# Cross-attention with state tokens and a SiLU feed-forward on one core: the instruction order of batch 0 rearranged

## The chip, the cores and the metric

The kernel runs on one core of a Trainium2 chip. Its engines are TensorE (PE: matmuls and transposes through an identity), VectorE (DVE), ScalarE (ACT: SiLU, exponentials, copies), GpSimd (POOL) and SyncE (SP, which issues transfers here). The metric is the device time of one execution in microseconds (us), lower being better. Nine runs of the kernel before gave a median of 216.46 us, from 216.35 to 216.77.

## The reference, cut to what matters

```python
# B, H, S, Ns, D = 8, 8, 512, 32, 64;  w_in 512 x 2048, w_out 2048 x 512, all float32
scores = (x @ state.T) / 8                    # per batch and head
xread  = softmax(scores) @ state              # 512 rows a batch
sread  = softmax((state @ x.T) / 8) @ x       # 32 rows a batch
y = concat([xread, sread], axis=2)            # 544 rows a batch, heads side by side: 512 wide
h = y @ w_in
out = (h * sigmoid(h)) @ w_out                # 4352 rows of 512
```

## The kernel before, in words

**Two products are folded.** For the 512 xread rows of a batch the kernel never forms xread. It multiplies the state into `w_in` once a batch (`W1`, `w1_mms`, line 449: 32-row pieces of four heads packed into the 128 rows of an output, for two groups of heads), and then h = W1 x softmax. `W1[b]` has two groups (`hg`) of 128 x 2048 bf16. A `w1_mms` for 512 columns is eight small matmuls into two PSUM banks; `w1_out` (471) copies the two banks to SBUF, by the two engines given (`both` is DVE for group 0, ACT for group 1).

**Tiles.** `d_ff` has 16 blocks of 128, called steps `ft`. G1 of step ft (`emit_G1`, 523; step number k = 16 b + ft; `g1_first`, 489, for the very first) is two 512-wide matmuls of W1 and the transposed softmax `aT`, into one of two PSUM banks of the pool `psH`, and one SiLU on ACT that writes `g`. G2 (548) adds `g` of a step times `w_out` into the output of one of four token tiles `tt`, 16 steps each. Each output has a PSUM bank: tiles 0 and 1 of batch 0 have `o0` and `o1`, tiles 2 and 3 have `a0` and `a1`. `store` (564) copies a finished output to SBUF and sends it off. G1 of step 1 alone borrows `a1` (line 512). `bank()` (74) hands out the tags in the list `banks` in turn; for W1 pieces in batch 0 these are `a2` and `a3`. A buffer that is asked for again makes PE wait until its reader is done.

**Order.** Nothing is scheduled by a planner: each engine runs its instructions in the order in which the program emits them. `upto(k)` (592) emits G1 up to step k. In batch 0, loop at 643, `LEAD0` says how far G1 runs ahead of G2, and `W0` gives the steps at which W1 of batch 0 gets its next 512 columns; `ready` limits G1 to columns that exist. Steps 5 and 9 make columns 0 to 511 and 512 to 1023 of batch 1's W1 (652); step 4 places batch 1's state (650). G2 of tile 3 runs with the others for steps 0 to 2, then stops; three of its steps are issued at step 12 and the rest from 685 on, as PE's work while batch 1's softmax is made. That softmax: `cast_x` (127) makes x bf16 in `x_rows`, `pe_transpose_x` (243) transposes it on PE, `scores` (297), `exps` (312, ACT), `norm` (369: sum and reciprocal on DVE, product on POOL for group 0 and on DVE for group 1), `pe_transpose_a` (393). After it come the last two W1 pieces of batch 1 and its G1.

**The start.** x of batch 0 comes in two loads on SP. Its second half (heads 4 to 7) is cast by ACT (row groups c 2, 3) and POOL (c 0, 1) at 268 and 269. `keep_busy` (161) emits idle matmuls. ACT must load a table of functions before the first EXP and before the first SiLU; the instruction on `warm` before a section brings the load forward.

**Loads.** Weights, states and x of batches 1 to 3 are issued by POOL, in program order with POOL's own work.

From line 700 on, batches 1 to 7 follow in a loop, and then the 256 sread rows.

Of the kernel before, what the change touches and what calls it, by code (L numbers as in the profile page):

```python
# [9 lines left out]
BF16 = mybir.dt.bfloat16  # L10
# [15 lines left out]
NFT = DF // 128  # L26
# [15 lines left out]
def kernel(  # L42
# [8 lines left out]
    nc = tc.nc  # L51
# [75 lines left out]
    def cast_x(b, eng, c0=0, nc_=4, h0=0, nh=H):  # L127
        if b < 2:
            x_nat[b] = padded(b)
        elif b not in x_nat:  # L130
            x_nat[b] = xpool.tile([128, 4, 4, 128], BF16, tag="x_nat", name=f"x_nat{b}")
        copy(
            eng,
            x_nat[b][:, ds(c0, nc_), ds(h0 // 2, nh // 2), :].rearrange(
                "p c k (u d) -> p c k u d", u=2
            ),
            x_f[b % 2][:, ds(h0, nh), ds(c0, nc_), :].rearrange("p (k u) c d -> p c k u d", u=2),
        )
# [12 lines left out]
    def load_w_out(g0, n):  # L151
        nc.gpsimd.dma_start(w_out_sb[:, ds(g0, n), :], wout_re[:, ds(g0, n), :])

    def copy(eng, dst, src):
        if eng is nc.scalar:
            nc.scalar.activation(dst, src, func=COPY, bias=0.0)  # L156
        else:
            eng.tensor_copy(dst, src)  # L158


    def keep_busy(n, pool, tag):
        ps = pool.tile([128, 512], FP32, tag=tag, name="ps_busy")
        for _ in range(n):
            nc.tensor.matmul(  # L164
                ps[:], busy[:, 0:128], busy[:], start=True, stop=True, skip_group_check=True
            )
# [36 lines left out]
    def transpose_one_state(st):  # L203
        ps = bank([128, 2, 2, 2, 16], BF16, "ps_st1")
        nc.tensor.transpose(
            ps.rearrange("p g k u m -> p (g k u m)"), st.rearrange("p v d -> p (v d)"), ident[:]
        )
        return ps
# [8 lines left out]
    def place_one_state(b, ps, eng):  # L217
        for u in range(2):
            by_n = slots_of(b)[u].rearrange("p g (k m v) -> p g k m v", m=16, v=2)
            for v in range(2):  # L220
                copy(eng, by_n[:, :, 0:3:2, :, v], ps[ds(64 * v, 64), :, :, u, :])
# [21 lines left out]
    def pe_transpose_x(b, hg, nb=2, new=bank, engs=(nc.vector, nc.scalar), only=None):  # L243
        if b not in xT:
            xT[b] = xtpool.tile([128, 4, 4, 128], BF16, tag="xT", name=f"xT{b}")
        m = 4 // nb
        for u in range(nb) if only is None else only:
            ps = new([128, m, 2, 128], BF16, "ps_xt")
            for i in range(m):
                for j in range(2):  # L250
                    nc.tensor.transpose(  # L251
                        ps[:, i, j, :],
                        x_nat[b][:, m * u + i, 2 * hg + j, :],
                        ident[:],
                    )
            copy(engs[u], xT[b][:, ds(m * u, m), ds(2 * hg, 2), :], ps[:])
# [9 lines left out]
    o_tags = ["o0", "o1"]  # L266
    new_o = lambda sh, dt, nm: psO.tile(sh, dt, tag=o_tags.pop(), name=nm)
    cast_x(0, nc.scalar, 2, 2, 4, 4)
    cast_x(0, nc.gpsimd, 0, 2, 4, 4)
    pe_transpose_x(0, 0, 2, new_o, (nc.vector, nc.vector))  # L270

    st_x = pers.tile([128, 8, B, 4, 2, 2], BF16)

# [116 lines left out]
            aT[b][:, hg, :, :], an[b, hg][:].rearrange("p c s n -> p (c s n)")  # L390
        )

    def pe_transpose_a(b, hg, eng, new=bank, c0=0, n=4):
        ps = new([128, n, 128], BF16, "ps_at")
        for c in range(n):
            nc.tensor.transpose(ps[:, c, :], an[b, hg][:, c0 + c, :, :], ident[:])
        copy(eng, aT[b][:, hg, ds(c0, n), :], ps[:])


    xm_ps = {}  # L400
# [48 lines left out]
    def w1_mms(b, cols, new=bank):  # L449
        pss = {}  # L450
        if b not in W1:
            W1[b] = wpool.tile([128, 2, DF], BF16, tag="W1", name="W1")
        for f, n in cols:
            for hg in range(2):
                pss[f, hg] = new([128, 512], FP32, "ps_w1")
            for s in range(4):
                for hg in range(2):
                    h = HEAD_OF_SLOT[hg][s]
                    r = 64 * (h % 2)
                    nc.tensor.matmul(  # L460
                        pss[f, hg][ds(32 * s, 32), 0:n],
                        stT[ds(r, 64), b, h // 2, s % 2, :],
                        w_in_sb[ds(r, 64), h // 2, ds(f, n)],
                        start=True,
                        stop=True,
                        tile_position=(r, 32 * s),
                        skip_group_check=True,
                    )
        return pss

    def w1_out(b, cols, engs, pss, at=0):
        for f, n in cols:
            for hg in range(2):
                copy(engs[hg], W1[b][:, hg, ds(f + at, n)], pss[f, hg][:, ds(at, n)])

    def w1_cols(b, cols, engs, new=bank):
        w1_out(b, cols, engs, w1_mms(b, cols, new))
# [114 lines left out]
    def upto(k):  # L592
        while done[0] < min(k, (B + 1) * NFT):
            emit_G1(done[0])
            done[0] += 1

    new_h = lambda sh, dt, nm: psH.tile(sh, dt, tag="h1", name=nm)
    keep_busy(1, psH, "h1")
    scores(0, 0)
    exps(0, 0)  # L600
    keep_busy(1, psH, "h1")
    pe_transpose_x(0, 1, 2, new_h, (nc.vector, nc.scalar))
    norm(0, 0)
    scores(0, 1, 2)
    exps(0, 1)
    norm(0, 1, ((nc.vector, 0, 4),), 2)
    pss0 = w1_mms(0, [(0, 128)])
    nc.scalar.activation(warm[:], busy[:, 0:1], func=SILU, bias=0.0)
    w1_out(0, [(0, 128)], (nc.scalar, nc.scalar), pss0)
    load_w_in(1024)  # L610
    load_w_out(8, 4)
    load_w_in(1536)
    for hg in range(2):
        load_x(1, 4 * hg, 4)
    load_w_out(12, 4)
    load_states()
    load_x(2)
    for i in range(3):
        ones_beside_x(i, nc.gpsimd)
    keep_busy(3, psH, "h1")  # L620
    pss0 = w1_mms(0, [(128, 384)])
    keep_busy(2, psH, "h1")
    new_o = lambda sh, dt, nm: psO.tile(sh, dt, tag=o_tags.pop(), name=nm)
    o_tags[:] = ["o0", "o1"]
    for c in (0, 2):
        pe_transpose_a(0, 0, nc.scalar, new_o, c, 2)
    for c in (0, 2):
        pe_transpose_a(0, 1, nc.vector, bank, c, 2)
    upto(1)
    w1_out(0, [(128, 128)], (nc.vector, nc.vector), pss0)  # L630
    w1_out(0, [(128, 256)], (nc.vector, nc.vector), pss0, 128)
    upto(2)

    banks[:] = ["a2", "a3"]
    turn[0] = 0
    W0 = {2: (512, 512), 6: (1024, 512), 10: (1536, 512)}
    LEAD0 = [2, 2, 2, 2, 2, 3, 2, 3, 3, 2, 2, 4, 4]  # L640
    F3 = 3
    ready = 4
    for ft in range(NFT - 2):
        upto(min(ft + LEAD0[min(ft, 12)], ready))
        if ft in W0:
            w1_cols(0, [W0[ft]], both)
            ready = sum(W0[ft]) // 128
        if ft == 4:
            place_one_state(1, transpose_one_state(st1_n), nc.vector)
        if ft in (5, 9):  # L650
            w1_chunks(1, ({5: 0, 9: 1}[ft],), both)
        if ft == 11:
            for hg in range(2):
                cast_x(1, nc.vector, 0, 4, 4 * hg, 4)
            load_x(3)
        if ft == 12:
            nc.scalar.activation(warm[:], busy[:, 0:1], func=EXP, bias=0.0)
            for i in range(F3, F3 + 3):
                G2(0, 3, i)
            pe_transpose_x(1, 0, 1, engs=(nc.vector,))  # L660
            pe_transpose_x(1, 1, 1, engs=(nc.vector,))
        for tt in range(4 if ft < F3 else 3):
            G2(0, tt, ft)
    F3 += 3
    banks[:] = ["a2", "a3", "a0", "a1"]
    turn[0] = 0
    scores(1, 0, new=new_h)
    scores(1, 1, new=new_h)
    exps(1, 0)
    exps(1, 1)  # L670
    for tt in (0, 2, 1):
        G2(0, tt, 14)
        G2(0, tt, 15)
        if tt != 1:
            store(0, tt, nc.scalar)
    nc.scalar.activation(warm[:], busy[:, 0:1], func=SILU, bias=0.0)
    norm(1, 0)
    norm(1, 1, ((nc.vector, 0, 4),))
    tail_tags = ["a2", "a3", "a0", "o0"]

    def tail_bank(shape, dtype, name):
        tag = tail_tags.pop(0)
        return (psO if tag == "o0" else psA).tile(shape, dtype, tag=tag, name=name)

    for ft in range(F3, NFT):
        if ft == 12:
            pe_transpose_a(1, 0, nc.vector, new_h)
        if ft == 14:
            pe_transpose_a(1, 1, nc.vector, new_h)
            store(0, 1, nc.vector)  # L690
            cols = [(1024, 512), (1536, 512)]
            pss1 = w1_mms(1, cols, tail_bank)
            w1_out(1, cols, (nc.vector, nc.vector), pss1)
            for i in (2, 3):
                for c in range(4):
                    cast_x(i, nc.gpsimd, c, 1)
            transpose_states()
            transpose_x(2)
            upto(NFT + 2)
        G2(0, 3, ft)  # L700
    upto(NFT + 3)
    store(0, 3, nc.vector)

# [100 lines left out]
```

The softmax here doesn't subtract the row's maximum and nothing guards it: scores larger than these inputs give would overflow.

## Time and profile before

| what | value |
|---|---|
| median of nine runs | 216.46 us |
| the profiled execution | 216.41 us |
| its span, first to last instruction | 214.6 us |
| granted TensorE clock, mean | 1.000 |
| PE busy | 205.5 us (96%), 1549 instructions |
| ACT busy | 139.6 us (65%), 244 instructions |
| DVE busy | 76.5 us (36%), 170 instructions |
| POOL busy | 39.6 us (18%), 61 instructions |
| G2 outside of `o_a`, 128x512 | 483 records, mean 379 ns |
| G1 of batches 0 to 7, 128x512 | 242 records, mean 379 ns |
| SiLU and its forms | 143 records, mean 573 ns |
| table loads on ACT | 1283 ns each |

The profile is of one execution. Matmuls are pipelined, so that the 379 ns of one are not the time from one to the next; a few per cent of the matmul records are missing. "Slices" are the span cut into 40 equal parts, each digit the busy share in tenths. The "chain" goes back from the last instruction to what released it, and so on. A "hole" in this text is time on PE in which no matmul started that could have.

### The profile page before, as it was taken

The numbers are of one execution on the slowest core, as the hardware profiler recorded it, in microseconds if no ns is written. First come the engines' busy times: TensorE is split into PE (matmuls) and PEld (weight loads), VectorE is DVE, ScalarE is ACT, GpSimd is POOL, SyncE is SP. The second block draws the span as 40 slices with busy tenths as digits, with TensorE's granted clock in tenths as the row PEclk, the third lists the DMA queues.
The fourth block names the chain that finished last, engine by engine and source line by source line (L and its number), as shares of the span: only waits on it lengthen the run. The fifth ranks groups of instructions, "written<-read, shape, count | busy, mean of one in ns | idle before, by whom it ended". The sixth has DMA issues, their size and how long they took to land.

```text
span 214.6 us, 3867 instructions
## 1 busy us (share of the span) xinstructions
PE 205.5 (96%) x1549; PEld 96.8 (45%) x1575; DVE 76.5 (36%) x170; ACT 139.6 (65%) x244; POOL 39.6 (18%) x61
## 2 busy tenths in 40 slices
PE   7899999999899999999999999999999999999993
PEld 2443344445344444444444444444444444466653
DVE  3734247855951156106610551135312415200011
ACT  3866578699657976699459956786675366634410
POOL 8683013702420122004110402000200000000000
PEclk9999999999999999999999999999999999999999
DMA  5999999696649567374657295114310211011112
GB/s 187 206 202 206 293 273 340 172 234 214 89 99 264 157 107 195 88 208 105 167 80 240 76 156 127 49 52 104 94 53 16 91 49 53 0 49 49 52 49 98
DMA packets 42914, 28.66 MB, mean 134 GB/s; under 512 B 28048, under 2 KB 37776, under 8 KB 42896
## 3 DMA queue, kind: packets, MB, share of 16 engines
q1 hardware_dynamic: 36720, 20.65, 37.3%
q0 software_dynamic: 5888, 7.64, 17.1%
q8 instruction: 12, 0.20, 0.4%
q10 hardware_dynamic: 288, 0.13, 0.2%
q14 instruction: 6, 0.05, 0.1%
HBM read 17.43 MB, written 8.91 MB: 123 GB/s over the span
## 4 chain that ended last, share of the span: by engine, by line
PE 86%; DVE 5%; ACT 3%; DMA 2%; issue 1%; POOL 0%; POOLq 0%
PE o L555 47%; PE h L514 25%; PE ps_w L460 4%; PE h L535 3%; PE o_a L555 2%; DMA x_f<-in_x_dram 2%; PE o_part L577 2%; DVE W L158 2%; ACT exp_nat L317 1%; DVE rs L376 1%; PE ps_xt L251 1%; PE ps_sr L412 1%; DVE rc L428 1%; PE ps_scT L329 1%; ACT L317 1%
## 5 line engine op out<-in xcount | busy, mean ns | idle before, releaser
L555 PE MATMUL o<-w_out_sb,g 128*128 128x512 bf16 x483 | 129.3, 379 | 1.8 <-issue 1.1
L546 ACT ACTIVATE g<-h 128x512 bf16<-128x512 f32 (+1 forms) x143 | 81.4, 573 | 37.0 <-PE h L514 23.0
L555 PEld LDWEIGHTS <-g 128*128 128x128 bf16 x528 | 50.0, 98 | 57.6 <-issue 3.2
L514 PE MATMUL h<-aT,W 128*128 128x512 bf16 x242 | 72.2, 379 | 0.5 <-ACT g L546 0.3
L158 DVE COPY o_sb<-o 128x512 f32<-128x512 f32 x15 | 10.4, 691 | 89.2 <-PE o L555 85.1
L514 PEld LDWEIGHTS <-W 128*128 128x128 bf16 x254 | 24.5, 98 | 31.8 <-issue 2.0
L158 DVE CAST W<-ps_w 128x512 bf16<-128x512 f32 (+2 forms) x37 | 23.0, 648 | 25.3 <-PE ps_w L460 25.3
L156 ACT ACTIVATE W<-ps_w 128x512 bf16<-128x512 f32 (+1 forms) x31 | 16.4, 570 | 12.6 <-PE ps_w L460 12.6
L158 POOL CAST x_nat<-x_f 128x512 bf16<-128x512 f32 x24 | 14.6, 650 | 33.6 <-issue 22.7
L156 ACT ACTIVATE o_sb<-o 128x512 f32<-128x512 f32 x16 | 9.6, 597 | 12.1 <-PE o L555 8.9
L359 POOL TENSOR_TENSOR an<-e,rcn 128x512 bf16<-128x512 bf16 x5 | 7.6, 1519 | 49.1 <-DVE rcn L357 49.1
L460 PE MATMUL ps_w<-w_in_sb,stT 64*32 64x512 bf16 (+2 forms) x264 | 11.1, 375 | 0.7 <-DVE W L158 0.7
L555 PE MATMUL o_a<-w_out_sb,g 128*128 128x512 bf16 x32 | 10.2, 379 | 0.1
L535 PE MATMUL h<-xmT,w_in_sb 128*128 128x256 bf16 x64 | 9.6, 273 | 0.0
L535 PEld LDWEIGHTS <-w_in_sb 128*128 128x128 bf16 x64 | 6.3, 98 | 3.9
L164 PE MATMUL ps_busy<-busy 128*128 128x512 bf16 x15 | 5.7, 487 | 1.2 <-DVE warm L171 1.2
L460 PEld LDWEIGHTS <-stT 64*32 64x32 bf16 x264 | 3.4, 89 | 7.3 <-issue 4.9
L748 ACT ACT_TABLE_LOAD x5 | 6.4, 1283 | 0.1
L343 ACT ACTIVATE eT<-ps_scT 128x512 bf16<-128x512 f32 x10 | 5.4, 595 | 1.6 <-PE ps_scT L329 1.6
L379 POOL TENSOR_TENSOR an<-exp_nat,rc 128x512 bf16<-128x512 bf16 x3 | 3.1, 1050 | 17.6 <-ACT eT L343 10.7
L356 DVE TENSOR_REDUCE rs<-e 128x32 f32<-128x1024 bf16 x5 | 6.1, 1211 | 0.2 <-DMA e<-eT 0.2
L108 POOL DMA_DIRECT2D x_f<-in_x_dram x4 | 3.3, 841 | 12.5 <-DVE x_rows L158 10.3
(76 smaller groups left out, 104.0 us busy)
## 6 DMA issues: line engine op xcount, KB each, us to landing
out_dram<-o_sb SPq DMA_DIRECT2D x33, 256.0 KB, 2.4
x_f<-in_x_dram SPq DMA_DIRECT2D x4, 1024.0 KB, 6.3
x_f<-in_x_dram POOLq DMA_DIRECT2D x2, 1024.0 KB, 13.5
w_in_sb<-in_moe_w_in_dram POOLq DMA_DIRECT2D x3, 512.0 KB, 10.5
w_out_sb<-in_moe_w_out_dram POOLq DMA_DIRECT2D x3, 512.0 KB, 12.3
x_f<-in_x_dram SPq DMA_DIRECT2D x2, 512.0 KB, 4.9
x_f<-in_x_dram POOLq DMA_DIRECT2D x2, 512.0 KB, 15.2
w_out_sb<-in_moe_w_out_dram POOLq DMA_DIRECT2D x2, 256.0 KB, 7.8
```

The costliest lines, as they stand in the source:

```text
L156: nc.scalar.activation(dst, src, func=COPY, bias=0.0)
L158: eng.tensor_copy(dst, src)
L164: nc.tensor.matmul(ps[:], busy[:, 0:128], busy[:], start=True, stop=True, skip_group_check=True)
L343: nc.scalar.activation(t[:, hg], scT_ps[hg][:], func=EXP, bias=0.0, scale=SCALE)
L356: nc.vector.tensor_reduce(rs[:], e2[b][:], axis=AX, op=ADD)
L359: eng.tensor_tensor(a[:, hg], e2[b][:, hg], rc[:, hg].to_broadcast([128, 4, 4, NS]), op=MULT)
L460: nc.tensor.matmul(pss[f, hg][ds(32 * s, 32), 0:n], stT[ds(r, 64), b, h // 2, s % 2, :], w_in_sb[ds(r, 64), h // 2, ds(f, n)], start=True, ...
L514: nc.tensor.matmul(h_ps[k][:], W1[b][:, hg, ds(128 * ft, 128)], aT[b][:, hg, :, :], start=(hg == 0), stop=(hg == 1), skip_group_check=True,)
L535: nc.tensor.matmul(ps[:, 0:256], w_in_sb[:, kt, ds(128 * ft, 128)], xmT[:, :, kt].rearrange("p t n b -> p t (n b)"), start=(kt == 0), stop ...
L546: nc.scalar.activation(g[:, 0:n], ps[:, 0:n], func=SILU, bias=0.0)
L555: nc.tensor.matmul(outs[tt][:], gt[b * NFT + ft][:, ds(128 * tt, 128)], w_out_sb[:, ft, :], start=(ft == 0), stop=(ft == NFT - 1), skip_gr ...
L748: nc.scalar.activation(warm[:], busy[:, 0:1], func=SILU, bias=0.0)
```

## The change

The order and the buffers of batch 0, and of the passage to batch 1, are rewritten:

- POOL casts row group 0 of the second half of x, DVE row group 1 (in its queue between the first two and the third copy to `xT`), ACT groups 2 and 3 as before.
- ACT copies the first 128 columns of W1 ahead of its load of the SiLU table. The next pieces use banks `a2` and `a3`; the transposed softmax of batch 0 uses `o1`, `a0`, `a1`, `o0`, and its copies, and those of W1 columns 128 to 255, are shared by DVE and ACT.
- The last load of `w_out` is issued as two.
- Batch 1's state is placed at step 1. W1 of batch 1 gets columns 0 to 511 at step 4, and 512 to 1023 at step 6, directly behind batch 0's piece; the latter goes into the two `psH` banks.
- G2 of tile 3 starts at the end of step 1 and keeps up to step 6; steps 7 to 11 stand between the transposes and scores of batch 1, 12 and 13 between the transposes of its softmax, 14 and 15 behind its first two G1.
- The last piece of batch 0's W1 is at step 10. At step 11 come G1 12 and 13, the casts and first transposes of x of batch 1, G1 14 and 15, and the EXP table. Tiles 0 to 2 do steps 12 to 15 behind the scores, in twos, tile by tile.

From the sums over batch 1 on, the program is the same. The diff, cut to its core:

```diff
     cast_x(0, nc.scalar, 2, 2, 4, 4)
-    cast_x(0, nc.gpsimd, 0, 2, 4, 4)
+    cast_x(0, nc.gpsimd, 0, 1, 4, 4)
     pe_transpose_x(0, 0, 2, new_o, (nc.vector, nc.vector))
+    cast_x(0, nc.vector, 1, 1, 4, 4)
...
-    pss0 = w1_mms(0, [(0, 128)])
+    w1_cols(0, [(0, 128)], (nc.scalar, nc.scalar))
     nc.scalar.activation(warm[:], busy[:, 0:1], func=SILU, bias=0.0)
-    w1_out(0, [(0, 128)], (nc.scalar, nc.scalar), pss0)
...
-    load_w_out(12, 4)
+    load_w_out(12, 2)
+    load_w_out(14, 2)
...
     keep_busy(3, psH, "h1")
+    banks[:] = ["a2", "a3"]
+    turn[0] = 0
     pss0 = w1_mms(0, [(128, 384)])
     keep_busy(2, psH, "h1")
...
     for c in (0, 2):
-        pe_transpose_a(0, 0, nc.scalar, new_o, c, 2)
+        ps_a = (psO, psA)[c // 2].tile(
+            [128, 2, 128], BF16, tag=("o1", "a0")[c // 2], name="ps_at"
+        )
+        at_mms(ps_a, 0, 0, c, 2)
+        copy(both[c // 2], aT[0][:, 0, ds(c, 2), :], ps_a[:])
     for c in (0, 2):
-        pe_transpose_a(0, 1, nc.vector, bank, c, 2)
+        ps_a = (psO, psA)[c == 0].tile(
+            [128, 2, 128], BF16, tag=("o0", "a1")[c == 0], name="ps_at"
+        )
+        at_mms(ps_a, 0, 1, c, 2)
+        copy(nc.vector, aT[0][:, 1, ds(c, 2), :], ps_a[:])
+    w1_out(0, [(128, 128)], both, pss0)
     upto(1)
-    w1_out(0, [(128, 128)], (nc.vector, nc.vector), pss0)
...
-    LEAD0 = [2, 2, 2, 2, 2, 3, 2, 3, 3, 2, 2, 4, 4]
-    F3 = 3
+    W1_AT = {4: 0, 6: 512}
+    LEAD0 = [2, 2, 2, 2, 2, 3, 2, 1, 3, 3, 2, 3]
+    T3 = {1: (0, 1), 2: (2,), 3: (3,), 4: (4,), 5: (5,), 6: (6,)}
...
-    for ft in range(NFT - 2):
-        upto(min(ft + LEAD0[min(ft, 12)], ready))
+    for ft in range(12):
+        upto(min(ft + LEAD0[ft], ready))
+        if ft == 1:
+            place_one_state(1, transpose_one_state(st1_n), nc.vector)
         if ft in W0:
-            w1_cols(0, [W0[ft]], both)
+            pss = w1_mms(0, [W0[ft]])
+            if ft in W1_AT:
+                pss1 = w1_mms(1, [(W1_AT[ft], 512)], new_h)
+            w1_out(0, [W0[ft]], both, pss)
+            if ft in W1_AT:
+                w1_out(1, [(W1_AT[ft], 512)], both, pss1)
             ready = sum(W0[ft]) // 128
-        if ft == 4:
-            place_one_state(1, transpose_one_state(st1_n), nc.vector)
-        if ft in (5, 9):
-            w1_chunks(1, ({5: 0, 9: 1}[ft],), both)
+        elif ft in W1_AT:
+            w1_cols(1, [(W1_AT[ft], 512)], both)
         if ft == 11:
             for hg in range(2):
                 cast_x(1, nc.vector, 0, 4, 4 * hg, 4)
             load_x(3)
-        if ft == 12:
+            pe_transpose_x(1, 0, 1, engs=(nc.vector,))
+            upto(16)
             nc.scalar.activation(warm[:], busy[:, 0:1], func=EXP, bias=0.0)
-            for i in range(F3, F3 + 3):
-                G2(0, 3, i)
-            pe_transpose_x(1, 0, 1, engs=(nc.vector,))
-            pe_transpose_x(1, 1, 1, engs=(nc.vector,))
-        for tt in range(4 if ft < F3 else 3):
+        for tt in range(3):
             G2(0, tt, ft)
...
+            if ft == 7 and tt == 0:
+                upto(9)
+        for i in T3.get(ft, ()):
+            G2(0, 3, i)
+    pe_transpose_x(1, 1, 1, engs=(nc.vector,))
+    G2(0, 3, 7)
     scores(1, 0, new=new_h)
+    for ft in range(8, 12):
+        G2(0, 3, ft)
     scores(1, 1, new=new_h)
     exps(1, 0)
     exps(1, 1)
-    for tt in (0, 2, 1):
-        G2(0, tt, 14)
-        G2(0, tt, 15)
-        if tt != 1:
-            store(0, tt, nc.scalar)
+    for fts in ((12, 13), (14, 15)):
+        for tt in (0, 2, 1):
+            for ft in fts:
+                G2(0, tt, ft)
+            if fts[1] == 15 and tt != 1:
+                store(0, tt, nc.scalar)
...
+    pe_transpose_a(1, 0, nc.vector, new_h)
+    G2(0, 3, 12)
+    pe_transpose_a(1, 1, nc.vector, new_h)
+    G2(0, 3, 13)
...
-    for ft in range(F3, NFT):
-        if ft == 12:
-            pe_transpose_a(1, 0, nc.vector, new_h)
-        if ft == 14:
-            pe_transpose_a(1, 1, nc.vector, new_h)
...
+    upto(NFT + 2)
+    G2(0, 3, 14)
+    G2(0, 3, 15)
     upto(NFT + 3)
```

More of the change, by code (lines that the diff above doesn't have):

```diff
@@ L391, in transpose_a, with at_mms, pe_transpose_a @@
         )
-    def pe_transpose_a(b, hg, eng, new=bank, c0=0, n=4):
-        ps = new([128, n, 128], BF16, "ps_at")
+    def at_mms(ps, b, hg, c0=0, n=4):
         for c in range(n):
             nc.tensor.transpose(ps[:, c, :], an[b, hg][:, c0 + c, :, :], ident[:])
-        copy(eng, aT[b][:, hg, ds(c0, n), :], ps[:])
+    def pe_transpose_a(b, hg, eng, new=bank):
+        ps = new([128, 4, 128], BF16, "ps_at")
+        at_mms(ps, b, hg)
+        copy(eng, aT[b][:, hg, :, :], ps[:])
     xm_ps = {}
@@ L597 @@
     new_h = lambda sh, dt, nm: psH.tile(sh, dt, tag="h1", name=nm)
+    new_o = lambda sh, dt, nm: psO.tile(sh, dt, tag=o_tags.pop(), name=nm)
     keep_busy(1, psH, "h1")
@@ L601 @@
     keep_busy(1, psH, "h1")
-    pe_transpose_x(0, 1, 2, new_h, (nc.vector, nc.scalar))
+    pe_transpose_x(0, 1, 2, new_h, both)
     norm(0, 0)
@@ L620 @@
     keep_busy(3, psH, "h1")
+    banks[:] = ["a2", "a3"]
+    turn[0] = 0
     pss0 = w1_mms(0, [(128, 384)])
     keep_busy(2, psH, "h1")
-    new_o = lambda sh, dt, nm: psO.tile(sh, dt, tag=o_tags.pop(), name=nm)
-    o_tags[:] = ["o0", "o1"]
     for c in (0, 2):
-        pe_transpose_a(0, 0, nc.scalar, new_o, c, 2)
-    for c in (0, 2):
-        pe_transpose_a(0, 1, nc.vector, bank, c, 2)
+        ps_a = (psO, psA)[c // 2].tile(
[3 more added lines that the diff above has]
+        copy(both[c // 2], aT[0][:, 0, ds(c, 2), :], ps_a[:])
+    for c in (0, 2):
+        ps_a = (psO, psA)[c == 0].tile(
[4 more added lines that the diff above has]
+    w1_out(0, [(128, 128)], both, pss0)
     upto(1)
-    w1_out(0, [(128, 128)], (nc.vector, nc.vector), pss0)
     w1_out(0, [(128, 256)], (nc.vector, nc.vector), pss0, 128)
     upto(2)
-    banks[:] = ["a2", "a3"]
     turn[0] = 0
     W0 = {2: (512, 512), 6: (1024, 512), 10: (1536, 512)}
-    LEAD0 = [2, 2, 2, 2, 2, 3, 2, 3, 3, 2, 2, 4, 4]
-    F3 = 3
+    W1_AT = {4: 0, 6: 512}
+    LEAD0 = [2, 2, 2, 2, 2, 3, 2, 1, 3, 3, 2, 3]
+    T3 = {1: (0, 1), 2: (2,), 3: (3,), 4: (4,), 5: (5,), 6: (6,)}
     ready = 4
-    for ft in range(NFT - 2):
-        upto(min(ft + LEAD0[min(ft, 12)], ready))
+    for ft in range(12):
+        upto(min(ft + LEAD0[ft], ready))
+        if ft == 1:
+            place_one_state(1, transpose_one_state(st1_n), nc.vector)
         if ft in W0:
-            w1_cols(0, [W0[ft]], both)
+            pss = w1_mms(0, [W0[ft]])
[4 more added lines that the diff above has]
+                w1_out(1, [(W1_AT[ft], 512)], both, pss1)
             ready = sum(W0[ft]) // 128
-        if ft == 4:
-            place_one_state(1, transpose_one_state(st1_n), nc.vector)
-        if ft in (5, 9):
-            w1_chunks(1, ({5: 0, 9: 1}[ft],), both)
+        elif ft in W1_AT:
+            w1_cols(1, [(W1_AT[ft], 512)], both)
         if ft == 11:
@@ L655 @@
             load_x(3)
-        if ft == 12:
+            pe_transpose_x(1, 0, 1, engs=(nc.vector,))
+            upto(16)
             nc.scalar.activation(warm[:], busy[:, 0:1], func=EXP, bias=0.0)
-            for i in range(F3, F3 + 3):
-                G2(0, 3, i)
-            pe_transpose_x(1, 0, 1, engs=(nc.vector,))
-            pe_transpose_x(1, 1, 1, engs=(nc.vector,))
-        for tt in range(4 if ft < F3 else 3):
-            G2(0, tt, ft)
-    F3 += 3
-    banks[:] = ["a2", "a3", "a0", "a1"]
-    turn[0] = 0
+        for tt in range(3):
+            G2(0, tt, ft)
+            if ft == 7 and tt == 0:
[4 more added lines that the diff above has]
+    G2(0, 3, 7)
     scores(1, 0, new=new_h)
+    for ft in range(8, 12):
+        G2(0, 3, ft)
     scores(1, 1, new=new_h)
@@ L678 @@
     norm(1, 1, ((nc.vector, 0, 4),))
+    pe_transpose_a(1, 0, nc.vector, new_h)
+    G2(0, 3, 12)
+    pe_transpose_a(1, 1, nc.vector, new_h)
+    G2(0, 3, 13)
+    banks[:] = ["a2", "a3", "a0", "a1"]
+    turn[0] = 0
     tail_tags = ["a2", "a3", "a0", "o0"]
@@ L683, in tail_bank @@
         return (psO if tag == "o0" else psA).tile(shape, dtype, tag=tag, name=name)
-    for ft in range(F3, NFT):
-        if ft == 12:
-            pe_transpose_a(1, 0, nc.vector, new_h)
-        if ft == 14:
-            pe_transpose_a(1, 1, nc.vector, new_h)
[L690 to L700, printed above, removed]
+    store(0, 1, nc.vector)
+    w1_cols(1, [(1024, 512), (1536, 512)], (nc.vector, nc.vector), tail_bank)
+    for i in (2, 3):
+        for c in range(4):
+            cast_x(i, nc.gpsimd, c, 1)
+    transpose_states()
+    transpose_x(2)
+    upto(NFT + 2)
+    G2(0, 3, 14)
+    G2(0, 3, 15)
     upto(NFT + 3)
```

## The prediction

> **What bounds it now.** I read the page's slices first, then the chain of waits, then the timelines of 10 to 40 us, then the DMA landings.
>
> ```profile
> PE   7899999999899999999999999999999999999993
> ACT  3866578699657976699459956786675366634410
> PEclk9999999999999999999999999999999999999999
> DMA  5999999696649567374657295114310211011112
> ```
>
> After two slices (5.4 us each) TensorE is 90% or more busy almost to the end, at full clock: the kernel is a queue of matmuls, and only holes in that queue can be won. A 9 can hide half a us. The diff works in slices 1 to 7; DMA is full there too, so I must ask whether PE runs into its landings. The chain names the holes:
>
> ```profile
> 20.38 0.69 DVE W L158
> 21.08 0.04 issue
> 21.12 0.55 PE ps_w L460 x8
> 21.67 0.69 DVE W L158
> ...
> 27.11 0.69 DVE W L158
> ...
> 28.49 0.61 ACT g L546
> ...
> 35.68 1.06 POOL an L379
> 36.73 0.05 issue
> 36.78 0.40 PE ps_at L396 x4
> ```
>
> Each line that is not PE is a time at which PE had nothing ready. Their sizes come from the PE timeline (start, us, what). A 512-wide matmul starts every 0.216 us when nothing is missing (two of h and one of o fill 0.65 us at 43.65, 44.30, 44.95 in the chain); what goes beyond is a hole.
>
> ```profile
> 13.05 0.79 PE L555 MATMUL o_a<-w_out_sb,g 128*128 128x512 bf16 x2
> 26.63 0.41 PE L460 MATMUL ps_w<-w_in_sb,stT 64*32 64x512 bf16 x8
> 26.97 0.60 PE L555 MATMUL o<-w_out_sb,g 128*128 128x512 bf16 x2
> ...
> 37.76 0.63 PE L460 MATMUL ps_w<-w_in_sb,stT 64*32 64x512 bf16 x16
> 38.32 0.82 PE L514 MATMUL h<-aT,W 128*128 128x512 bf16 x3
> ```
>
> First line: two matmuls in 0.79 instead of 0.59, a hole of 0.20. The others give the price of a W1 piece: one piece holds PE for 0.34 (26.63 to 26.97) plus 0.10 to enter, two in a row 0.56 plus 0.10.
>
> **The change, part by part.** Number and widths of matmuls stay. After batch 0 everything on every engine is in the old order, so I compare one event: the first h of batch 1, at 38.32 now. From the first G2 (12.62) to it are 25.70 us.
>
> (1) *Fourth tile from step 1.* At step 0, G2 of tile 3 wanted bank a1, held by h of step 1 until its SiLU ended at 13.42: the 0.20 above. It is now issued at the end of step 1, long after. Gain 0.20. Its matmuls only move forward.
>
> (2) *W1 of batch 1 with batch 0's.* Five single pieces (steps 2, 5, 6, 9, 10) become three (2, 4, 10) and a pair (6): 5 x 0.44 against 3 x 0.44 + 0.66. Gain 0.22. The pieces at 5 and 6 used the same banks, so the second waited for DVE's eviction: it began 0.44 after the o_a before it at 20.68 instead of 0.31, and held 0.42 instead of 0.34. Gain 0.21. The batch-1 state must be placed before step 4; its transpose and four copies (0.97 of DVE) move to step 1, about 13.6 to 14.5, into a DVE idle of 3.00 us; its load lands at 4.50 + 7.5 = 12.0. Nothing is queued behind it that PE needs.
>
> (3) *What the joined pair costs.* It uses both h banks. DVE evicts batch 0's half (0.69), then batch 1's (about 0.6), so the first bank is free 0.47 + 0.69 + 0.6 + 0.05 = 1.82 after the pair starts. PE has the pair (0.56) and five G2 (1.09) = 1.65: G1 of step 8 waits 0.17. Before, a W1 eviction cost 0.21 there (21.98 to 22.41). Gain 0.04. Bounds: free if two DVE copies overlap by 0.17 more, 0.4 if ACT's copies are late behind a SiLU; I take the sum. G1 8's SiLU comes later, but two G2 and one G1 lie ahead of its first reader.
>
> (4) *W1 wait at step 10 to 11* (27.41 to 27.85, 0.22): piece and three G2 are the same. No gain.
>
> (5) *G1 12 to 15 behind the last piece.* Three in a row with two h banks meant a wait for SiLU: 28.51 to 29.14 is 0.63, a hole of 0.42. Now the order is two G1, eight transposes (0.45), two G1. SiLU 12 is done about when the transposes end; SiLUs follow each other at 0.49 (1.09 for two), so G1 15 waits 0.08. Gain 0.34. The cast that feeds the transposes is DVE's 0.68 after the W eviction, done about 0.3 ahead.
>
> (6) *Batch-1 softmax.* Now exp, sum, reciprocal and multiply end at 36.73 on POOL, and PE, out of tile-3 work, waits 0.24 (36.33 to 36.78). Worked forward: PE reaches scores of group 1 about 32.6 and has twelve G2 (2.6) until 35.4. ACT ends SiLU 15 at 31.0, loads EXP (1.28), first exp 32.35 to 32.95, the second follows its scores to 33.6. From the first reduce, POOL's product ends 2.18 later (34.55 to 36.73) and DVE's 2.72 later (to 37.27): 35.2 and 35.7. PE asks at 35.4 and, after transposes and one G2, 35.8. Gain 0.24, with 0.1 to 0.2 to spare: the tightest point. SiLU's load falls at 35.8 to 37.1, before the first SiLU of batch 1 (37.5).
>
> (7) *The start.* ACT copies the first W1 columns before its SiLU load, so they no longer stand between load and aT copies; ACT and DVE share aT and W. Adding rows (aT copy 0.29 DVE, 0.39 ACT; W 0.28; 0.1 to PE): aT pieces ready 11.22, 11.53, 11.60, 11.73, W for h 1 at 11.93, so h 1 starts 12.04 instead of 12.17. Gain 0.14. W1 of columns 128 on now uses bank a2 and waits for ACT's copy, 0.05, absorbed by idle matmuls.
>
> The cast of x by three engines is meant to hand PE its transposes before 7.37. POOL's half becomes about 0.35, DVE's new piece about 0.29 (512 wide took 0.43). Run side by side from the landing at 1.27 + 5.4 = 6.67, both are done by 7.06, PE starts at 7.22 and 0.15 is won down the chain. The nearest row says otherwise:
>
> ```profile
> 36.67 1.06 POOL L158 CAST x_nat<-x_f 128x512 bf16<-128x512 f32 x1
> 38.25 0.61 POOL L158 CAST x_nat<-x_f 128x512 bf16<-128x512 f32 x1
> ```
>
> The same cast takes 1.06 when DVE's product of two SBUF operands runs beside it (36.39 to 37.27), 0.61 beside DVE's evictions from PSUM. The Trainium skill (SBUF — State Buffer, "Who interferes with whom") says that a DVE cast from SBUF to SBUF in a two-port mode and a GpSimd instruction share an exclusive port pair, and the later one waits until the other is done. No row here has that very pair. By the rule: 6.70 + 0.35 + 0.29 = 7.34, against 7.31 now: gain 0. By the side-by-side sum: 0.15. I take 0; the row is near enough.
>
> (8) *POOL's queue.* One w_out load becomes two, one more issue (0.75) ahead of the state load, x of batch 2 and the memsets, all idle-covered: x of batch 2 lands at 35.6 and is cast after 35.2.
>
> Sum: 0.20 + 0.22 + 0.21 + 0.04 + 0.34 + 0.24 + 0.14 = 1.39.
>
> **Do the loads allow it?** us from issue to landing:
>
> ```profile
> w_in_sb<-in_moe_w_in_dram POOLq DMA_DIRECT2D x1, 512.0 KB, 10.5
> w_in_sb<-in_moe_w_in_dram POOLq DMA_DIRECT2D x1, 512.0 KB, 14.1
> x_f<-in_x_dram POOLq DMA_DIRECT2D x1, 512.0 KB, 15.6
> ```
>
> Issued at 10.26, 11.80 and 13.28: they land at 20.76, 25.9 and 28.9. My forward sum asks for the first at 21.3 (step 6), the second at 26.65 (step 10), the third through DVE's cast at 30.8. Slack 0.5, 0.7 and 1.2. The last w_out lands at 31.2 at the latest and is wanted at 32.8. So landings don't bind, and I cost them at nothing; each us later than the slack costs one. x of batch 3 is still issued at 29.9 and lands at 39.0, so POOL ends its casts at 41.5 as now; its transpose lands near 46, wanted at 49.8. Hence batch 1 keeps the whole 1.39.
>
> The profiled execution took 216.41 (span 214.64 and 1.77 around it), the median is 216.46. 216.41 - 1.39 = 215.02; on the median 215.07. I say 215.1.
>
> **Rivals.** (a) *Holes that I left close too*: no port lock (-0.15), G1 8's and G1 15's waits vanish (-0.25): 214.7. For it: the landing of x may come apart so that the casts don't collide. (b) *The softmax wait returns*: PE has only twelve G2 and one to hide it, now that tile 3 is used up early, and 0.1 of slack; if ACT reaches EXP 0.5 later, or the joined pair and start give nothing, half of a us is lost: 215.6. Against: every duration is a row of this trace. (c) *The loads bind*: DMA is full, and PE arrives earlier; with w_in 1.8 later all is lost: 216.4. Against: the order of the loads up to x of batch 1 is unchanged. (d) *Slower: x of batch 1 lands late.* Both casts stand on DVE ahead of the first xT copy, and PE, in order, stands at the second transposes with nothing behind them able to pass; softmax and all G1 of batch 1 follow. Price: landing + 0.75 - 30.8, so one us per us after 30.05; it eats the gain at 31.4 and makes the kernel slower by 0.2% from 31.9, 3 us later than now; at 32.2, 217.2. Before, PE wanted the same data no earlier than 31.3. Against: no new load stands ahead of it.
>
> **Chances.** Forecast 50%, (a) 18%, (b) 22%, (c) 5%, (d) 5%. Faster and slower mean more than 0.2% (0.43 us), about what a measurement can tell from no change. (a), (b) and the forecast are all faster, 0.90; (c) is 0.05, (d) 0.05. Forecast alone: 214.9 to 215.35. The range takes in (a) and most of (b): 214.65 to 215.9.
>
> **What would show it.** Right: first h of batch 1 near 36.9; no DVE W line in the chain near 20 to 22, no POOL an line near 35; a double W1 block near 21.3; PE of the later batches unchanged. The transposes of the second half of x at 7.35 confirm the lock, at 7.2 refute it. Wrong: a DMA line before L460, or x_rows waiting for x_f with PE behind it; an ACT exp or DVE an line in the chain at 33 to 36; a lower clock in the first slices.

## The result and the profile after

The changed kernel took 214.9 us (median of 10 runs, 214.43 to 215.09) against 216.48 for the kernel before (32 runs): ratio 0.9918, 95% interval 0.9907 to 0.9928. That is 0.2 below the forecast of 215.1 and inside its range. The profiled execution took 215.09, with a span of 213.3.

The slices of the changed kernel, as they answer to those of before (TensorE, then ACT, clock and DMA):

```profile
PE   7799999999899999999999999999999999999993
...
ACT  2866677899467876697569955885775367644410
...
PEclk9999999999999999999999999999999999999999
DMA  5999999993749358454747675114311211011112
```

PE's row is as full as it was; half a us of holes in a slice of 5.3 us can hide in a 9. The chain of waits shows the change. It lists start, length, engine, tile and line; here it is cut to the places that were rearranged:

```profile
21.22 0.43 PE o_a L559 x2
21.65 0.56 PE ps_w L464 x16
22.21 0.54 PE o L559 x2
...
23.39 0.22 PE h L518
...
27.26 0.69 DVE W L158
...
28.00 1.04 PE h L518 x4
29.03 0.45 PE ps_xt L251 x8
29.48 0.89 PE h L518 x4
...
35.60 0.22 PE ps_at L396 x4
```

Of the five waits that before's chain had in this stretch, two for DVE's W copies at 20 to 22, one at 27, one for a SiLU at 28.5 and one for POOL's product at 35.7, only that at 27 is left. The double W1 piece (21.65) is followed by G2 at once, and the softmax transposes (35.60) come in their turn in PE's queue.

To compare executions I use three events on PE: the first transpose of the second half of x, the first G2, and the first h of batch 1. The third row is a second profile of the changed kernel (label c_after), taken beside the kernel before on one chip.

| kernel | x, 2nd half | first G2 | first h, batch 1 | transposes to G2 | G2 to h of batch 1 | h of batch 1 to the end |
|---|---|---|---|---|---|---|
| before | 7.37 | 12.62 | 38.32 | 5.25 | 25.70 | 176.32 |
| after | 7.71 | 12.75 | 36.96 | 5.05 | 24.21 | 176.35 |
| c_after | 7.51 | 12.56 | 36.77 | 5.05 | 24.21 | 176.35 |

So the change wins 0.20 between the transposes and the first G2, 1.49 up to the first h of batch 1, and nothing after: 1.69. c_after's median was 1.70 below before's; the medians of the first comparison, 214.9 and 216.48, differ by 1.58. The first profile of the changed kernel shows only 1.36 at the first h, because its transposes of x began 0.34 later than before's; the last section comes back to that.

### The profile page after: what moved, and what is told of

Same layout as the page of the kernel before. It is cut to its first block, busy times and chain, and to the rows that moved or that the text cites. A ratio compares the mean times of both kernels' runs of the same rounds, so it can differ in the third digit from the quotient of the medians.

```text
span 213.3 us, 3870 instructions
## 1 busy us (share of the span) xinstructions
PE 204.8 (96%) x1549; PEld 96.6 (45%) x1575; DVE 77.0 (36%) x171; ACT 139.5 (65%) x244; POOL 40.0 (19%) x62
## 4 chain that ended last, share of the span: by engine, by line
PE 89%; DVE 5%; DMA 2%; ACT 1%; issue 1%
PE o L559 48%; PE h L518 25%; PE ps_w L464 4%; PE h L539 3%; PE o_a L559 3%; DMA x_f<-in_x_dram 2%; PE o_part L581 2%; DVE W L158 1%; PE ps_sr L416 1%; PE ps_xt L251 1%; DVE rc L432 1%; PE ps_sc L304 1%; PE ps_busy L164 1%; PE ps_scT L330 1%; ACT L318 1%
## 5 line engine op out<-in xcount | busy, mean ns | idle before, releaser
L559 PE MATMUL o_a<-w_out_sb,g 128*128 128x512 bf16 x30 | 9.4, 379 | 0.1
L432 DVE RECIPROCAL rc<-ps_sr 32x2 f32<-32x2 f32 x32 | 5.2, 164 | 0.3
```

Of the source, the lines that this page charges most:

```text
L432: nc.vector.reciprocal(rc[q, :], src)
L559: nc.tensor.matmul(outs[tt][:], gt[b * NFT + ft][:, ds(128 * tt, 128)], w_out_sb[:, ft, :], start=(ft == 0), stop=(ft == NFT - 1), skip_gr ...
```

## The experiments

Each was compared with the kernel before on the same chip, whose median was 216.30 to 216.42. "Stretch" is first G2 to first h of batch 1 in the profile (24.21 in the changed kernel).

| label | us | ratio (95%) | stretch |
|---|---|---|---|
| c_after | 214.72 | 0.9918 (0.9904–0.9931) | 24.21 |
| e1_cast_by_two | 214.63 | 0.9922 (0.9908–0.9935) | 24.21 |
| e2_start_alone | 216.27 | 0.9997 (0.9988–1.0006) | 25.70 |
| e3_pair_apart | 215.13 | 0.9942 (0.9929–0.9954) | 24.58 |
| e4_four_g1 | 215.23 | 0.9945 (0.9933–0.9958) | 24.66 |
| e5_tile3_at_0 | 214.80 | 0.9927 (0.9914–0.9939) | 24.41 |
| e6_fill_10 | 214.77 | 0.9923 (0.9910–0.9935) | 24.19 |
| e6b_fill_and_order | 214.39 | 0.9912 (0.9899–0.9924) | see below |
| e7_act_late | 215.09 | 0.9941 (0.9928–0.9953) | 24.71 |
| e8_casts_beside | 214.78 (one run) | – | 24.21 |
| e9_table_first | 215.15 | 0.9938 (0.9926–0.9950) | 24.21 |
| e10_one_idle_less | 214.25 | 0.9899 (0.9886–0.9912) | 24.00 |

**The control, c_after.** The changed kernel again.

> The changed kernel once more, for comparison with the three others on one chip. The time of 12.6 to 38.3 before (first G2 to first h of batch 1) was 25.70; it was 24.21 in two profiles of this order. Theory: 24.21 again, whatever the start does; the time differs from run to run by the start alone, where PE's matmuls take twice as long until some moment between 4 and 7 us and x lands between 4.99 and 5.34. Rival: the stretch itself varies by 0.1 or more.

It gave the row in the first table: the stretches agree with the first profile to 0.01, while the start moved by 0.2. Hence the experiments below are read by stretches first, and by times second.

**e1_cast_by_two.** The second half of x is cast by ACT and POOL alone, as before.

```diff
-    cast_x(0, nc.gpsimd, 0, 1, 4, 4)
+    cast_x(0, nc.gpsimd, 0, 2, 4, 4)
...
-    cast_x(0, nc.vector, 1, 1, 4, 4)
```

> The changed kernel with the cast of x's second half by two engines again (POOL both row groups, DVE none). Port lock as in the prediction: the split wins nothing, so the time stays at 214.9 (within 0.1), and PE's transposes of the second half begin at the same time. Side by side: the split wins 0.15, so this is 215.05 and the transposes begin 0.15 later. Third: something else than the casts (PE's own queue of idle matmuls) sets the start of the transposes; then nothing changes, and the trace shows an idle matmul directly ahead of them.

Measured: 214.63, ratio 0.9922, the same as the changed kernel. Transposes began 0.69 after the landing of x (told by the start of ACT's cast), as before (0.70). In the profiles with three engines it was 0.58 to 0.68 in five (e3, e5, e7, e9, e10) and 0.82 to 0.98 in the other seven. In those seven it is not a cast that PE waits for: all casts were done 0.17 to 0.24 earlier. PE itself comes late, since its first transposes ran late or slowly (see the last section) and the scores and an idle matmul stand between them and the second ones. In c_after DVE's cast, the last of the three, ends at 7.31, with the idle matmul on PE:

```profile
7.29 0.38 PE L164 MATMUL ps_busy<-busy 128*128 128x512 bf16 x1
7.51 0.61 PE L251 MATMUL ps_xt<-ident,x_rows 128*128 128x128 bf16 x8
```

So the split is worth some 0.1 at most, and only in executions in which PE is early.

**e2_start_alone.** The kernel before with the new start alone (casts, W copies ahead of the SiLU table, shared copies).

> The kernel before with the new start alone: casts by three, W1 copies ahead of the SiLU table, new banks and shared copies; from the first steps on the old order, and w_out in one load. Prediction's step 7: 0.14 faster than before, 216.35. Rival, from the profile of the changed kernel, in which the first G2 began at 12.75 instead of 12.62: the new start costs 0.14, 216.6, and all of the gain comes from the later steps.

The trace has transposes to G2 in 5.04 instead of 5.25, with 25.70 behind it as before, so 0.21 comes from the start. The time, 216.27, doesn't show it: its interval, 0.9988 to 1.0006, holds no gain and one of 0.2 alike. By time this run is inconclusive.

**e3_pair_apart.** The second piece of batch 1 goes back from step 6 to step 9, by itself.

```diff
-    W1_AT = {4: 0, 6: 512}
+    W1_AT = {4: 0, 9: 512}
```

> The changed kernel with batch 1's second W1 piece alone at step 9 in the two banks a2 and a3 instead of joined at step 6. Theory (entering and leaving a packed piece costs PE 0.22, and two pieces close together wait for DVE's eviction): 0.22 for the pair taken apart plus 0.2 for the wait between steps 9 and 10, so 0.4 slower than the changed kernel: 215.3. Rival, that only the wait counts: 215.1; that neither counts because the h banks lent to the pair held up G1 8: 214.9 or less.

Stretch +0.37, as expected. The W copy that the pair avoids is back in the chain:

```profile
25.84 0.69 DVE W L158
...
26.57 0.49 PE ps_w L464 x8
27.07 0.69 DVE W L158
```

**e4_four_g1.** G1 12 to 15 in a row, transposes behind them.

```diff
-            pe_transpose_x(1, 0, 1, engs=(nc.vector,))
             upto(16)
+            pe_transpose_x(1, 0, 1, engs=(nc.vector,))
```

> The changed kernel with G1 12 to 15 in a row, the transposes of x of batch 1 behind them. Theory (two h banks, SiLU every 0.49): a hole of about 0.42 before G1 14 and about 0.06 before G1 15 come back, less what was there: 0.4 slower, 215.3; the EXP table is loaded a little later and may add 0.1. Rival, that the hole only moves because the softmax of batch 1 sets the end of this stretch: the same time, 214.9, with the softmax reached with 0.4 less to wait for.

Stretch +0.45. PE stands behind a SiLU as it did before:

```profile
28.32 0.61 ACT g L550
28.93 0.04 issue
28.97 1.08 PE h L518 x4
```

**e5_tile3_at_0.** Tile 3 with step 0, as before the change.

```diff
-    T3 = {1: (0, 1), 2: (2,), 3: (3,), 4: (4,), 5: (5,), 6: (6,)}
+    T3 = {0: (0,), 1: (1,), 2: (2,), 3: (3,), 4: (4,), 5: (5,), 6: (6,)}
```

> The changed kernel with G2 of tile 3, step 0, at step 0 again, where its bank a1 is still held by h of step 1. Theory: PE waits 0.2 there for the SiLU of step 1, and the time is 0.2 more than the changed kernel's 214.7 to 214.9. Rival: the wait of W1 at step 2 (bank a2, state copies on DVE, or its load) takes it up, and nothing is lost.

Stretch +0.20: the two matmuls of `o_a` take 0.79 again, as in the first line of the prediction's PE timeline. In time the intervals overlap (ratio 0.9927 against c_after's 0.9918).

```profile
12.56 0.79 PE L559 MATMUL o_a<-w_out_sb,g 128*128 128x512 bf16 x2
```

**e6_fill_10 and e6b_fill_and_order.** At the one wait left in the chain, at 27.3, PE stands for 0.22, the time of one G2. Both move G2 of tile 3, step 7, into it; e6b also gives the softmax transposes back that time, by issuing G2 12 and 13 ahead of them.

```diff
-    T3 = {1: (0, 1), 2: (2,), 3: (3,), 4: (4,), 5: (5,), 6: (6,)}
+    T3 = {1: (0, 1), 2: (2,), 3: (3,), 4: (4,), 5: (5,), 6: (6,), 10: (7,)}
...
-    G2(0, 3, 7)
# e6b_fill_and_order alone
-    pe_transpose_a(1, 0, nc.vector, new_h)
     G2(0, 3, 12)
-    pe_transpose_a(1, 1, nc.vector, new_h)
+    pe_transpose_a(1, 0, nc.vector, new_h)
     G2(0, 3, 13)
+    pe_transpose_a(1, 1, nc.vector, new_h)
```

> The changed kernel with G2 of tile 3, step 7, moved from behind the second transposes of x to the end of step 10, where PE waits 0.22 for DVE's eviction of W1. Hole theory alone: 0.22 less than the changed kernel. Rival, the softmax of batch 1 has no slack: in the changed kernel its second half was asked for at 35.87, and DVE's product ended at 35.79; PE comes 0.22 earlier and waits 0.19 there; gain 0.03. I expect the rival: the hole reappears ahead of the transposes of the softmax.

> As the one before, and G2 of tile 3, steps 12 and 13, each one place earlier, ahead of the transposes of the first and of the second half of the softmax. If the softmax is what took the 0.22 back, these two places give it the time that it needs, and the whole 0.22 comes through: 0.2 less than the changed kernel, first h of batch 1 after 24.0 us from the first G2. If something else took it back, as the one before.

e6 moved the stretch by 0.02: the G2 filled the hole, and the time came back as waits for the softmax. In the changed kernel the two groups of transposes start 0.44 apart, as two G2 would; in e6 0.55 apart, later than their turn:

```profile
35.02 0.40 PE L396 MATMUL ps_at<-ident,an 128*128 128x128 bf16 x4
...
35.57 0.40 PE L396 MATMUL ps_at<-ident,an 128*128 128x128 bf16 x4
```

e6b keeps it: from the first 512-wide W1 piece to the first h of batch 1 it takes 21.25 against 21.47. Its time was 214.39 against 214.72 for c_after, on the same chip, with intervals that overlap. Its stretch, 24.09, isn't in the table, since in its profile the first `w_in` columns landed about 1 us late, which held up the start and which the chain names:

```profile
2.36 7.98 DMA w_in_sb<-in_moe_w_in_dram
10.35 0.04 issue
10.39 0.36 PE ps_w L464 x8
```

**e7_act_late.** One useless copy of 0.52 on ACT, ahead of the EXP table: is ACT the tight engine of the softmax, as part 6 of the prediction says?

```diff
+    late = pers.tile([128, 512], BF16)
...
             upto(16)
+            nc.scalar.activation(late[:], busy[:], func=COPY, bias=0.0)
             nc.scalar.activation(warm[:], busy[:, 0:1], func=EXP, bias=0.0)
```

> The changed kernel with one more ACT copy (128x512, about 0.5, of no use) ahead of the EXP table load. Prediction's step 6 gave the softmax 0.1 to 0.2 to spare, so 0.3 to 0.4 slower; the trace of the changed kernel shows 0.15 for the first and 0.03 for the second half, so 0.45 slower. If ACT has time in hand there, nothing.

Stretch +0.50. Counted from the first G2, the first transposes of the softmax moved by 0.38 and the second by 0.49, so 0.14 and 0.03 of ACT's 0.52 were covered. The chain runs from SiLU 15 over the whole softmax to PE:

```profile
29.33 1.08 ACT g L551 x2
30.41 0.52 ACT late L677
...
30.95 1.28 ACT L678
...
34.09 1.05 POOL an L381
35.14 0.05 issue
35.19 0.40 PE ps_at L397 x4
```

**e8_casts_beside.** Is there a lock between DVE's casts and POOL's? Four useless casts on DVE, from SBUF to SBUF, beside four of POOL's; run once.

```diff
+    for _ in range(4):
+        nc.vector.tensor_copy(spare[:], x_f[0][:, 0:2].rearrange("p h c d -> p (h c d)"))
```

> The changed kernel with four more casts (SBUF to SBUF, float32 to bf16, 128x512, of no use) on DVE behind its evictions of W1 near 39 us, beside POOL's casts of x of batches 2 and 3. Lock: one waits for the other; POOL casts that meet one take 0.8 to 1.05 instead of 0.61, or the DVE casts 0.6 to 1.0 instead of 0.43. No lock: 0.61 and 0.43 as everywhere. The time of the kernel should stay, since neither is waited for within 2 us.

They overlap by the records, but neither keeps its speed. POOL's four:

```profile
38.94 2.86 POOL L158 CAST x_nat<-x_f 128x512 bf16<-128x512 f32 x4 [1.32 <-DMA x_f<-in_x_dram]
```

and DVE's:

```profile
39.31 2.77 DVE L719 CAST spare<-x_f 128x512 bf16<-128x512 f32 x4
```

In the same place c_after has 2.29 for POOL's four casts (0.61 for one), and a DVE cast of this shape at the start takes 0.43 alone. Here POOL's first cast, which meets DVE's only at its end, takes 0.62 and the other three 0.80 each; DVE's first takes 0.53, the others 0.71. Once both are at it, either engine begins a cast every 0.75 (POOL at 39.50, 40.25, 41.00), where POOL in c_after begins one every 0.56. They slow to one pace, which fits taking turns; side by side POOL would have kept its 2.29. But the eight were done in 3.1 and not in 2.29 + 4 x 0.43 = 4.0, so an engine is not shut out for the whole length of the other's record. DVE's four casts alone were not run.

**e9_table_first.** The SiLU table goes back ahead of ACT's copies of the first W1 columns, all else as changed.

```diff
-    w1_cols(0, [(0, 128)], (nc.scalar, nc.scalar))
+    pss0 = w1_mms(0, [(0, 128)])
     nc.scalar.activation(warm[:], busy[:, 0:1], func=SILU, bias=0.0)
+    w1_out(0, [(0, 128)], (nc.scalar, nc.scalar), pss0)
```

> The changed kernel with ACT's load of the SiLU table ahead of its copies of the first W1 columns again, the new banks kept. Prediction's step 7: the order saves ACT's time only, and its loss is 0.1 to 0.2. Rival: with the new banks the next W1 matmuls on PE want bank a2, which these very copies free; then PE stands until the table is loaded, and the loss is about 1.2.

Transposes to G2 took 5.41 instead of 5.05, 0.36 more. Neither number expected: the aT transposes now wait for the bank that ACT's late W copy reads.

```profile
10.30 0.28 PE L396 MATMUL ps_at<-ident,an 128*128 128x128 bf16 x2
10.86 0.55 PE L396 MATMUL ps_at<-ident,an 128*128 128x128 bf16 x6 [0.28 <-ACT W L156]
```

**e10_one_idle_less.** e6b, and one idle matmul less ahead of the transposes of x's second half.

```diff
     exps(0, 0)
-    keep_busy(1, psH, "h1")
     pe_transpose_x(0, 1, 2, new_h, both)
```

> The kernel with the hole of step 10 filled and the two G2 moved, and without the idle matmul ahead of the transposes of the second half of x. In the changed kernel's profiles that matmul was still running when the casts were done, so the split of the cast could not count. If it hid a gain: 0.1 to 0.15 less than with it, 214.25. If ACT's cast of its half (0.63 from the landing) sets the start anyway: nothing. It could also cost, if PE reaches its full rate later for want of work.

214.25 (214.22 to 214.32), stretch 24.00: the fastest here, 2.1 below the kernel before on its chip. Its gain over the changed kernel in the stretch, 0.21, is e6b's. Whether the idle matmul cost anything stays open: without it the transposes began 0.58 after the landing of x, as in the early profiles, but from there to the first G2 it took 5.12 instead of 5.05, and one start can't be told from the scatter of the others. Against c_after, on another chip, the intervals of the ratio still touch.

## Why the prediction was right, point by point

The form of the forecast held: seven holes on PE, summed, and everything from batch 1 on carried along unchanged (176.35 against 176.32). The sizes:

| step | predicted | measured | from |
|---|---|---|---|
| 1 tile 3 from step 1 | 0.20 | 0.20 | e5, stretch +0.20 |
| 2 pieces joined, bank wait gone | 0.43 | 0.43 | double piece at 0.56, no hole before; e3 gives 0.37 back |
| 3 G1 of step 8 behind the pair | 0.04 | 0.21 | no hole there |
| 4 wait of step 10 to 11 | 0 | 0 | still 0.22 in the chain |
| 5 G1 12 to 15 split | 0.34 | 0.39 | e4 +0.45; hole left 0.03 |
| 6 softmax wait | 0.24 | 0.24 | no hole |
| 7 start | 0.14 | 0.20 | 5.05 against 5.25; e2 5.04 |
| sum | 1.39 | 1.67 | whole: 1.69 |

The gains of steps 3 and 6 are read from the traces alone; no run takes them back one by one. The sum was 0.3 short of the 1.69 between the events. That the median came within 0.2 of the forecast is in part luck: 216.48 - 1.69 is 214.8. (Two small slips change nothing: the terms of step 3 add up to 1.81, not 1.82, and 12.17 to 12.04 in step 7 is 0.13.)

**Step 3 is the term that was mis-sized, by 0.17.** The prediction said that "the first bank is free 0.47 + 0.69 + 0.6 + 0.05 = 1.82 after the pair starts", which is DVE's second copy. Before, G1 8 stood 0.21 behind the last G2 (0.43 from start to start instead of 0.22):

```profile
21.98 0.38 PE L555 MATMUL o_a<-w_out_sb,g 128*128 128x512 bf16 x1
22.41 1.04 PE L514 MATMUL h<-aT,W 128*128 128x512 bf16 x4
```

In the changed kernel DVE's copy did end at about the time predicted. But G1 8 got the bank that ACT empties. ACT and DVE from 22 on:

```profile
22.09 1.09 ACT L156 ACTIVATE W<-ps_w 128x512 bf16<-128x512 f32 x2 [0.61 <-PE ps_w L464]
```

```profile
22.06 1.29 DVE L158 CAST W<-ps_w 128x512 bf16<-128x512 f32 x2 [2.35 <-PE ps_w L464]
```

ACT is done at 23.18, DVE at 23.35. PE starts G1 8 at 23.23, in its turn:

```profile
23.01 0.38 PE L559 MATMUL o<-w_out_sb,g 128*128 128x512 bf16 x1
23.23 0.38 PE L518 MATMUL h<-aT,W 128*128 128x512 bf16 x1
```

In the trace's records the first matmul of G1 8 waits for ACT's semaphore (the count by which ACT says that it is done), and that of G1 9, at 24.09, for DVE's. Handed out in strict turn, DVE's bank would have come first, and G1 8 would have stood until 23.40, the 0.17 predicted; why it got the other is not shown. The prediction had priced the right time for the wrong user.

**Step 5:** The four matmuls of G1 14 and 15 take 0.89 in the chain (four at 0.216 are 0.86), so 0.03 is left of the 0.08.

**Step 6** was right in its sum, and near its edge. POOL's product, DVE's, and the transposes on PE that want them:

```profile
34.19 1.04 POOL L380 TENSOR_TENSOR an<-exp_nat,rc 128x512 bf16<-128x512 bf16 x1 [3.86 <-DVE rc L378]
```

```profile
34.91 0.88 DVE L380 TENSOR_TENSOR an<-exp_nat,rc 128x512 bf16<-128x512 bf16 x1
```

```profile
35.43 0.39 PE L396 MATMUL ps_at<-ident,an 128*128 128x128 bf16 x4
...
35.87 0.39 PE L396 MATMUL ps_at<-ident,an 128*128 128x128 bf16 x4
```

POOL's product ends at 35.23 and PE comes at 35.43; DVE's ends at 35.79 and PE comes at 35.87. With 0.05 from a result to the matmul that uses it, the spare is 0.15 and 0.03, where the prediction had "0.1 to 0.2". e7 paid for ACT's delay beyond the first 0.03, and e6 lost its G2 to it. Rival (b) did not come, but it was 0.03 away, not 0.1.

**Step 7** was right for the table order and wrong in one cause. The prediction had W1 of columns 128 on wait 0.05 for ACT. By e9 it is the aT transposes that share their banks with the first W1 columns; since ACT's W copies come early in the changed kernel, nobody waits. That the cast of x by three engines is worth nothing held: e1 took it back at no cost. The test that the prediction named, transposes at 7.35 or 7.2, could not decide it: they began anywhere from 7.04 to 7.71 with the landing of x and PE's first rate. e5 shows the two casts meeting at the spot itself; POOL's 256 columns take 0.45 and DVE's 0.54 when they meet, against 0.40 and 0.28 in the changed kernel's first profile, where they don't:

```profile
6.51 0.45 POOL L158 CAST x_rows<-x_f 128x256 bf16<-128x256 f32 x1
```

```profile
6.58 0.54 DVE L158 CAST x_rows<-x_f 128x256 bf16<-128x256 f32 x1
```

Both are done by 7.12. By the Trainium skill's rule ("SBUF — State Buffer", "Who interferes with whom"), one behind the other, 6.51 + 0.40 + 0.28 is 7.19; side by side it would be 6.91. In e5 the rule is the nearer one. In e9, where POOL keeps its 0.40 (from 6.57) and DVE takes 0.48 (from 6.64), and in e8's longer row of casts the records lie between the two: the casts cost each other time, but less than the rule says. POOL alone with both groups (e1: 0.61) ends at 7.18.

**Loads and rivals.** The three loads landed at 20.1, 25.2 and 28.2. PE wanted the first two 1.5 later; DVE cast the third from 28.5 on, and PE transposed it at 30.85. So (c) and (d) had no part in it. (a) had two halves: its two G1 waits shrank (0.17 and 0.05 of its 0.25), its lock did not vanish. So the result lies between (a) and the forecast.

## What to carry to other kernels

On an in-order engine that is never idle for long, cost a reordering as a list of holes between two fixed events, and check it by the time between these events, which repeated here to 0.01 us while whole runs of the changed kernel scattered by 0.5 and more. Where buffers rotate, find out which instruction gets which buffer before pricing its wait: the pair's copies ended when they were expected to, but the first matmul behind it used the other bank. A filler moved into one hole must be looked for where it is missing: e6 won nothing until e6b also moved the transposes that it had covered.

## What the runs showed of the hardware that was not expected

**PE's first rate differs between executions.** Early matmuls take twice as long as later ones (0.107 instead of 0.056 per 128 columns), up to a moment that isn't the same in two executions of one program. Eight transposes of x in c_after, followed by the same eight in e1:

```profile
5.61 1.04 PE L251 MATMUL ps_xt<-ident,x_rows 128*128 128x128 bf16 x8
```

```profile
5.52 0.62 PE L251 MATMUL ps_xt<-ident,x_rows 128*128 128x128 bf16 x8 [0.38 <-DVE x_rows L158]
```

The clock row of the profile shows full speed throughout, but it misleads here. The clock records in the trace, from which it is made, begin only at the moment when the matmuls turn fast: at 3.89 in before, 5.13 and 7.14 in the two profiles of the changed kernel, and between 3.89 and 7.19 in all fourteen. The row counts the time ahead of the first record as full.

In six of the seven profiles with late second transposes of x this moment came at 6.18 or later; the seventh is the first profile of the changed kernel, in which x landed last. In the five with early ones it came at 3.97 to 5.64, or the idle matmul was left out (e10).

The Trainium skill ("TensorE: Matmul & The Clock Gate", Part 1) has PE begin at half rate and reach the full one about 4 us into sustained activity, give or take 0.5. Here it was 2.7 to 6.0 us after the first matmul at 1.19, so the half us does not hold. The records of full speed last 204.80, 208.21 or 211.63 us, which are 60, 61 and 62 times 3.413. So the clock seems to change on a beat of 3.41 us, and the earliest and latest moments, 3.30 apart, are about one beat from each other. This is read from these lengths; what sets the phase of the beat was not tried.

**Landings and one cast vary too.** x's second half landed between 6.45 and 6.78 (starts of ACT's cast). In after's first profile DVE's first cast of x took 0.72; in every other run here 0.43, like this one of c_after:

```profile
5.13 0.43 DVE L158 CAST x_rows<-x_f 128x512 bf16<-128x512 f32 x1 [1.26 <-DMA x_f<-in_x_dram]
```

Why it took 0.72 stays open. One thing sets it apart: it began 0.32 us into POOL's issue of a `w_in` load (5.02 to 5.81), while in the other profiles DVE's cast began at most 0.14 into that issue or ahead of it. Whether the two collide was not tried. With these, the first G2 came anywhere from 12.12 to 12.84, and a gain of 0.2 at the start, as in e2, can't be read from five runs' times.
